# Moving a diagonal sum and a turned gradient off TensorE, into the last phase of a fused layer's kernel

## The chip, the cores and the metric

The kernel runs on one core of one Trainium2 chip. The core has a matrix engine (TensorE, PE in the profile), a vector engine (VectorE, DVE), a scalar engine (ScalarE, ACT), GpSimd (POOL), and a sequencer (SyncE, SP) that here only issues DMA transfers. Weight loads of TensorE have a row of their own (PEld). Matrix products land in PSUM; everything else works on SBUF, a memory of 128 partitions. The metric is the device time of one execution in microseconds (us), and lower is better. The kernel before takes 1876.19 us, the median of three runs between 1875.66 and 1876.70.

## The reference

The function computes a layer and all of its gradients. The input is normalised, and the normalised rows `xn` go into two branches whose results are added to the input: a long convolution over time (branch A) and a gated MLP (branch B). The part that the change touches belongs to the gradients of branch A:

```python
# S = 2048 time steps, D = 1024 channels, ks = 4 taps
k_pad = jnp.pad(k, ((0, 0), (ks - 1, 0), (0, 0)))
for t in range(ks):
    k_shift = k_shift + k_pad[:, t:t + S, :] * shift_k[:, ks - 1 - t][None, None, :]
kv = k_shift * v
# y = causal convolution of kv with ssm_k (a filter of S steps for each channel), by FFT
y = y + kv * ssm_D[None, None, :]
return q * y
# [cut: layer norm, the MLP; jax.vjp gives the gradients of q, k, v, shift_k, ssm_k, ssm_D and the weights]
```

Two of these gradients matter here. Call `gks` the gradient that reaches `k_shift`, with S rows and D columns.

- **The gradient of `shift_k`** (D x 4): for each channel and each tap i it is the sum over time of `gks[t] * k[t - i]`. These are the tap sums.
- **The gradient of `ssm_k`** (D x S): a filter gradient, one row of 2048 time steps for each channel. Branch A works with time on the partitions and channels along the free axis, so this output has to be turned. Its element at time 0 is also the gradient of `ssm_D`.

## The kernel before

The kernel has four stretches. In the first three (`hidden`, `grad_down`, `grad_in`) TensorE does the MLP's products, and branch A is woven into them: a generator of slots puts a few of branch A's TensorE instructions between the MLP's at set distances, one group of 128 channels after another, eight groups in all. Then `out_phase` computes the output, and `grad_x` the gradient of the input, in 16 row tiles of 128 time steps each.

The tap sums before were matrix products. For each of 16 sub-rows and each block of 32 channels, TensorE multiplies a 128 x 32 piece of `gks` by four shifted pieces of `k`. Only the diagonals of the 32 x 32 results are wanted; VectorE masks them with an identity and sums them.

```python
def tap_sums(self, st):
    gks, kp = st["gks"], st["kp"]
    pd = self.banks("h x")[1](0)[:, 0:P].rearrange("p (i c) -> p i c", i=4)
    for r in range(16):
        for b in range(0, P, 32):
            self.mm(pd[b:b + 32], gks[:, r, b:b + 32], kp[:, r:r + 4, b:b + 32], start=(r == 0), stop=(r == 15))
    st["pd"] = pd

def tap_diagonals(self, st):
    dg = self.tmp.tile([P, 4, 32], F32, name="dg", tag="tmp")
    self.tt(dg[:], st["pd"], self.ident32[:].to_broadcast([P, 4, 32]), ALU.mult)
    self.pri.late()
    self.pri.pin(self.nc.vector.tensor_reduce(out=self.gs_all[:, st["gi"], :], in_=dg[:], axis=AX.X, op=ALU.add))
```

The last step of an inverse transform exists in two forms. `inv_b` leaves time on the partitions: its stationary operand is the small table `RB`. `inv_b_chan` leaves channels on the partitions, so that the filter gradient can be stored as the output wants it: its stationary operand is the data, 32 pieces of 128 x 128.

```python
def inv_b(self, st, key, half):
    dst, Cf = self.ttile(key), self.flp[:, half]
    for j in range(2):
        ps, at = self.banks("h r c", r=8)
        for q in range(4):
            for e in range(2):
                rows, n0 = slice(64 * e, 64 * e + 64), 16 * (q // 2) + 8 * j
                self.mm(at(e)[32 * q:32 * q + 32], self.RB[rows, e, :],
                        Cf[rows, n0:n0 + 8, 64 * (q % 2):64 * (q % 2) + 64])
        self.evict(...)                       # [cut: view]

def inv_b_chan(self, st, half):
    dst, Cf = self.ttile("ghn"), self.flp[:, half]
    for n0 in range(0, NB1, 16):
        ps, at = self.banks("h n c", n=8)
        for n in range(16):
            self.mm(at(n // 8)[:, n % 8, :], Cf[:, n0 + n, :], self.RB[:].rearrange("p h n -> p (h n)"))
        self.evict(...)                       # [cut: view]

def store_gh(self, st):                       # [cut: views]
    self.vcopy(self.gD_all[:, :, st["gi"]:st["gi"] + 1], ghv[0:64, :, 0:1])
    for b in range(2):
        self.store(self.out_gh[...], ghv[64 * b:64 * b + 64])
```

After the last group, `small_outputs` turns the collected tap sums and `ssm_D` gradients with six TensorE transposes and stores them. The last phase looks like this:

```python
def grad_x(self, ...):
    p_ev = tc.alloc_tile_pool(name="x_ev", bufs=2, side="right")
    for st in range(self.ST):                           # 16 row tiles
        ggT = self.tall(ug_d[:, 1, :], st, "ggT")       # DMA transposes; these two share a pool of three buffers
        guT = self.tall(ug_d[:, 0, :], st, "guT")
        # [cut: loads of gt, gy, xn on SP]
        V.tensor_tensor(out=gy[:], in0=gy[:], in1=gt[:], op=ALU.mult)
        if st == 1:
            self.rest_load(x, xn_d, y_d, Wd)
        gx, pr, w = ...                                 # pr: 128 x 1024 bf16, two buffers
        for ob in range(2):
            ps = self.ps_tile("ps_x")                   # a pool of four PSUM banks
            for T, W in ((ggT, self.wgT), (guT, self.wuT)):
                for kt in range(self.FT):               # 28
                    nc.tensor.matmul(ps, lhsT=T[:, kt, :], rhs=W[:, kt, oc], start=..., stop=...)
            V.tensor_tensor_reduce(out=gx[:, oc], in0=ps, in1=gy[:, oc], ...)
            V.tensor_tensor_reduce(out=pr[:, oc], in0=gx[:, oc], in1=xn[:, oc], ...)
            # [cut: row statistics]
        # [cut: ScalarE scales xn, VectorE adds, SP stores the row tile]
    self.rest_out(h_d, out0)                            # a short rest of the output's products
```

Of the kernel before, what the change touches and what calls it, by code (L numbers as in the profile page):

```python
# [11 lines left out]
BF16 = mybir.dt.bfloat16  # L12
F32 = mybir.dt.float32
I32 = mybir.dt.int32
ALU = mybir.AluOpType
ACT = mybir.ActivationFunctionType
AX = mybir.AxisListType
P = 128
# [3 lines left out]
class Pri:  # L22
# [4 lines left out]
    def __init__(self, tc):  # L27
        self.tc = tc
        self.n = 0
        self.strict = False  # L30
# [15 lines left out]
NB1 = 32  # L46


class ABranch:
# [4 lines left out]

    def __init__(self, tc, pri, S, D, k, v, g, shift_k, ssm_k, ssm_D, xn_d, y_d, sk_d, out_gk, out_gv, out_gsk,
                 out_gh, out_gsD):
        assert S == 2048 and D % P == 0
        self.tc, self.nc, self.pri = tc, tc.nc, pri
        self.S, self.D, self.NG = S, D, D // P
        self.k, self.v, self.g, self.shift_k, self.ssm_k, self.ssm_D = k, v, g, shift_k, ssm_k, ssm_D  # L60
        self.xn_d, self.y_d, self.sk_d = xn_d, y_d, sk_d
        self.out_gk, self.out_gv, self.out_gsk, self.out_gh, self.out_gsD = out_gk, out_gv, out_gsk, out_gh, out_gsD
        self.pools, self.pin, self.dense, self.queue = [], False, False, []
        self.cap, self.turns = 2, 0
# [83 lines left out]
    def tables(self):  # L148
        nc, con, big, pri = self.nc, self.con, self.big, self.pri
        pri.late()  # L150
        V, hold = nc.vector, self.tc.keep_in_program_order
# [4 lines left out]
        self.RB = con.tile([P, 2, NB1], BF16, name="RB")  # L156
        self.gs_all = con.tile([P, self.NG, 4], F32, name="gs_all")
        self.gD_all = con.tile([64, 2, self.NG], BF16, name="gD_all")
        negpi = con.tile([P, 1], F32, name="negpi")
# [23 lines left out]
        for a in range(2):  # L183
            V.tensor_scalar(out=it[:, a, :], in0=it[:, a, :], scalar1=b5[:], scalar2=32.0 * (1 + a) + 64.0,
                            op0=ALU.mult, op1=ALU.add)
# [6 lines left out]
        for ri in range(2):  # L192
            off = lin(b32, -1024.0, 1024.0 * (1 + ri) + 2048.0, "offF%d" % ri)
            q = big.tile([P, NB1, NB1], I32, name="qF", tag="big")
# [40 lines left out]

        self.ident32 = con.tile([P, 1, 32], BF16, name="ident32")
        self.NX = con.tile([1, 3, P], BF16, name="NX")
        V.memset(self.NX[:], 0.0)
        for b in range(0, P, 32):
            V.tensor_copy(out=self.ident32[b:b + 32, 0, :], in_=self.identA[b:b + 32, b:b + 32])  # L240

# [80 lines left out]
    def load_taps(self, st):  # L322
        skb = st["skb"] = self.sm.tile([P, 4, 1, P], BF16, name="skb")
        self.load(skb[:].rearrange("p i o c -> p (i o c)"),
                  self.sk_d[4 * st["gi"]:4 * st["gi"] + 4, :].rearrange("i c -> (i c)").partition_broadcast(P))
# [173 lines left out]

    def inv_b_chan(self, st, half):  # L500
        dst, Cf = self.ttile("ghn"), self.flp[:, half]
        st["ghn"] = dst
        dv = dst[:, 0:16, :].rearrange("p r c -> p (r c)").rearrange("p (n1 n2) -> p n1 n2", n2=NB1)
        for n0 in range(0, NB1, 16):
            ps, at = self.banks("h n c", n=8)
            for n in range(16):
                self.mm(at(n // 8)[:, n % 8, :], Cf[:, n0 + n, :], self.RB[:].rearrange("p h n -> p (h n)"))
            self.evict(ps, "p h n c -> p c (h n)", lambda s: dv[:, :, n0 + 8 * s.start:n0 + 8 * s.stop])
        yield

    def store_gh(self, st):
        ghf = st["ghn"][:, 0:16, :].rearrange("p r c -> p (r c)")
        ghv = ghf.rearrange("p (h t) -> p h t", h=2)
        self.vcopy(self.gD_all[:, :, st["gi"]:st["gi"] + 1], ghv[0:64, :, 0:1])
        for b in range(2):
            self.store(self.out_gh[st["cg"], 1024 * b:1024 * b + 1024].rearrange("(h c) t -> c h t", h=2),
                       ghv[64 * b:64 * b + 64])

    def halo(self, st):
# [4 lines left out]
        self.load(gks[P - 1:P, 16:19, :], self.NX[0:1, 0:3, :])  # L524

    def tap_sums(self, st):

        gks, kp = st["gks"], st["kp"]
        pd = self.banks("h x")[1](0)[:, 0:P].rearrange("p (i c) -> p i c", i=4)
        for r in range(16):  # L530
            for b in range(0, P, 32):
                self.mm(pd[b:b + 32], gks[:, r, b:b + 32], kp[:, r:r + 4, b:b + 32], start=(r == 0), stop=(r == 15))
        st["pd"] = pd

    def tap_diagonals(self, st):
        dg = self.tmp.tile([P, 4, 32], F32, name="dg", tag="tmp")
        self.tt(dg[:], st["pd"], self.ident32[:].to_broadcast([P, 4, 32]), ALU.mult)
        self.pri.late()
        self.pri.pin(self.nc.vector.tensor_reduce(out=self.gs_all[:, st["gi"], :], in_=dg[:], axis=AX.X, op=ALU.add))

# [32 lines left out]
    def steps(self):  # L573
# [25 lines left out]
        for st in self.sts:  # L599
            for p, d in (self.wide_slots if self.dense else self.slots)(st, st["gi"]):  # L600
# [8 lines left out]
                yield self.DENSE[p is None] if self.dense else self.SLOT  # L609
        self.small_outputs()  # L610

# [60 lines left out]
    def slots(self, st, gi):  # L672
# [56 lines left out]
        yield None, lambda: self.tt(gv[:, 0:16, :], gkv[:, 0:16, :], st["ksh"][:], ALU.mult)  # L729
        self.store_time(self.out_gv, st["cg"], gv)  # L730
        yield None, q
        yield None, self.both(lambda: self.halo(st), q)
        yield lambda: self.tap_sums(st), None
        self.fetch(nx, self.load_k, self.load_taps)
        f1g = None
        if not last:
# [3 lines left out]
            f1g = self.fwd1(self.Bg, nx["gt"])  # L740
        yield None, lambda: self.tap_diagonals(st)
        ia = self.inv_a_pair()
# [40 lines left out]
        yield None, tk  # L783
        yield self.inv_b_chan(st, 1), tk
        yield None, tk
# [19 lines left out]
    def wide_slots(self, st, gi):  # L805
# [60 lines left out]
        yield None, lambda: self.tt(gv[:, 0:16, :], gkv[:, 0:16, :], st["ksh"][:], ALU.mult)  # L866
        self.store_time(self.out_gv, st["cg"], gv)
        yield None, q
        yield None, self.both(lambda: self.halo(st), q)
        yield lambda: self.tap_sums(st), None  # L870
        self.fetch(nx, self.load_k, self.load_taps)
        f1g = None
        if not last:
# [3 lines left out]
            f1g = self.fwd1(self.Bg, nx["gt"])  # L877
        yield None, lambda: self.tap_diagonals(st)
        ia = self.inv_a_pair()
# [41 lines left out]
        yield None, tk  # L921
        yield self.inv_b_chan(st, 1), tk
        yield None, tk
# [18 lines left out]

    def small_outputs(self):
        nc, NG = self.nc, self.NG
        tp = nc.tensor.transpose
        sk = self.sm.tile([P, NG, 4], BF16, name="sk_o", bufs=1)
        self.vcopy(sk[:], self.gs_all[:])
        ps = self.ps.tile([P, 1024], BF16, name="ps8", tag="aps")
        for i in range(4):
            self.pri.now()  # L950
            self.pri.pin(tp(ps[0:NG, i * P:(i + 1) * P], sk[:, :, 3 - i], self.identA[:]))
        for h in range(2):
            self.pri.now()
            self.pri.pin(tp(ps[0:NG, 4 * P + 64 * h:4 * P + 64 * h + 64], self.gD_all[:, h, :], self.identA[0:64, 0:64]))
        so = self.tmp.tile([NG, 5, P], BF16, name="so", tag="tmp")
        self.vcopy(so[:, 0:4, :].rearrange("g i c -> g (i c)").rearrange("g (c i) -> g i c", i=4),
                   ps[0:NG, 0:4 * P].rearrange("g (i c) -> g i c", i=4))
        self.vcopy(so[:, 4, :], ps[0:NG, 4 * P:5 * P])
        self.store(self.out_gsk.rearrange("(g c) i -> g (c i)", c=P), so[:, 0:4, :].rearrange("g i c -> g (i c)"))
        self.store(self.out_gsD.rearrange("(g c) -> g c", c=P), so[:, 4, :])  # L960
A_START = 60_000


class LnMlp:
# [741 lines left out]

    def grad_x(self, x, g, xn_d, y_d, h_d, ug_d, Wd, out0, out1):
        nc, tc, D, V = self.nc, self.tc, self.D, self.nc.vector
        p_ev = tc.alloc_tile_pool(name="x_ev", bufs=2, side="right")
        p_sm = tc.alloc_tile_pool(name="x_sm", bufs=2, side="right")  # L1710
        for st in range(self.ST):
            for _ in range(6):
# [11 lines left out]
            if st == 1:  # L1724
                self.rest_load(x, xn_d, y_d, Wd)
            gx = p_ev.tile([P, D], F32, name="gx")
            pr = p_ev.tile([P, D], BF16, name="pr")
# [32 lines left out]
        self.rest_out(h_d, out0)  # L1760
        self.p_rest.release()
        p_sm.release()
        p_ev.release()
# [7 lines left out]
def kernel(  # L1771
# [32 lines left out]
    ug_d = dram.tile([S, 2, F], BF16, name="ug_d")  # L1804

    sk_d = dram.tile([D // P * 4, P], BF16, name="sk_d")

    pri = Pri(tc)
    b = LnMlp(tc, pri, S, D, F)
    a = ABranch(tc, pri, S, D, A_k[0], A_v[0], g, A_shift_k, A_ssm_k, A_ssm_D, xn_d, y_d, sk_d[:], out_2[0], out_3[0],  # L1810
                out_4, out_5, out_6)
    b.open_left()
# [36 lines left out]
    b.out_phase(x, xn_d, y_d, h_d, B_W_gate, B_W_up, out_0[0])  # L1849
    b.grad_x(x, g, xn_d, y_d, h_d, ug_d, B_W_down, out_0[0], out_1[0])  # L1850

# [29 lines left out]
```

## Time and profile before

| | value |
|---|---|
| time, median of three | 1876.19 us |
| span of the profiled execution | 1874.5 us |
| granted TensorE clock | 1.0 |
| branch A woven into the MLP's products | to about 1244 us |
| `out_phase` | 1290 to 1478 us |
| `grad_x` | 1478 us to the end |
| tap sums, TensorE instructions | 512 products of 128 x 32 by 128 x 128 |
| turned filter gradient, TensorE instructions | 256 products of 128 x 128 by 128 x 64 |
| `inv_b`, for two other results | 256 products of 64 x 32 by 64 x 512 |

The page of a profile gives the busy time of each engine first, then the span in forty slices, the DMA queues, the chain of work that ended last, and the costliest groups of instructions. A group's mean is the duration of one instruction as the profiler saw it. Matrix products are pipelined, so the durations of neighbours overlap, and the distance between the starts of two is what one of them costs. The timeline lists instructions in order of time with the start and the length of each run of like ones. The table by stretches gives, for each stretch, the busy time of each engine with the number of its instructions, the granted clock, the mean busy share of the sixteen DMA engines (it can exceed 1, since packets overlap) and the GB/s that they moved.

### The profile page before, as it was taken

Reading aid. Unit: us, or ns where it says so; the run is one execution under the profiler, and the core shown is the slowest. Engines: PE = TensorE matmul, PEld = TensorE weight load, DVE = VectorE, ACT = ScalarE, POOL = GpSimd, SP = SyncE. Lnnn points to the kernel's source line nnn. Section 1 sums busy time; section 2 is a strip of 40 time slices with the busy share of each in tenths; the row PEclk is TensorE's granted clock in tenths of the full one; section 3 lists DMA queues with packets and bytes.
Section 4 is the critical chain, followed back from the end, with each engine's and each line's share of the span. In section 5 each row is a group of like instructions: output and inputs, shape, how many; then the busy total and the mean of one; then the engine's idle time right before and its main releaser. Section 6 shows DMA issues by size and latency. Waiting matters only on the chain.

```text
span 1874.5 us, 32572 instructions
## 1 busy us (share of the span) xinstructions
PE 1852.7 (99%) x13478; PEld 852.5 (45%) x13707; DVE 1050.2 (56%) x1537; ACT 613.1 (33%) x904; POOL 14.8 (1%) x37
## 2 busy tenths in 40 slices
PE   9999999999999999999999999999999999999999
PEld 4444444444444444444444444444444544444444
DVE  6656888699698677685585876710222222222222
ACT  5745444534445445444535454320000000000000
POOL 1000000000000000000000000000000000000000
PEclk9999999999999999999999999999999999999999
DMA  9897499868568747377465353479999945555553
GB/s 254 257 246 169 134 204 222 193 166 200 150 163 209 246 100 192 104 185 216 136 148 153 97 165 98 136 172 278 259 226 249 249 115 123 124 123 124 124 124 73
DMA packets 695509, 323.72 MB, mean 173 GB/s; under 512 B 524864, under 2 KB 664896, under 8 KB 695360
## 3 DMA queue, kind: packets, MB, share of 16 engines
q1 hardware_dynamic: 684864, 300.78, 65.1%
q10 hardware_dynamic: 9216, 16.65, 2.9%
q0 software_dynamic: 1280, 4.20, 0.6%
q8 instruction: 107, 1.75, 0.4%
q14 instruction: 42, 0.34, 0.1%
HBM read 143.79 MB, written 95.44 MB: 128 GB/s over the span
## 4 chain that ended last, share of the span: by engine, by line
PE 97%; issue 1%; DMA 1%; DVE 0%; SPq 0%; ACT 0%; POOL 0%; ACTq 0%; POOLq 0%
PE ps_x L1739 21%; PE ps_w L1503 20%; PE ps_u L1171 10%; PE ps_h L1171 10%; PE ps_o L1670 10%; PE ps_g L1171 10%; PE ps_d L1503 9%; PE ps L89 4%; PE ps_d L1518 1%; PE ps_c L89 1%; PE ps_w L1518 1%; PE ps_r L1700 0%; PE ps_warm L1226 0%; DMA wu<-in_B_W_up_dram 0%; SPq L1189 0%
## 5 line engine op out<-in xcount | busy, mean ns | idle before, releaser
L1503 PE MATMUL ps_w<-ugs,xn_nat 128*128 128x512 bf16 x1672 | 377.1, 380 | 4.5 <-issue 2.4
L1171 PEld LDWEIGHTS <-xnT 128*128 128x128 bf16 x1792 | 170.8, 98 | 208.9 <-issue 8.2
L93 ACT CAST arena<-ps 128x1024 bf16<-128x1024 f32 x240 | 234.3, 1021 | 72.2 <-PE ps L89 62.9
L1503 PEld LDWEIGHTS <-xn_nat 128*128 128x128 bf16 x1728 | 164.4, 98 | 201.3 <-issue 9.8
L344 DVE STREAM_TRANSPOSE arena<-arena 128x1024 f32<-128x1024 f32 x96 | 180.4, 1933 | 129.1 <-ACT arena L93 115.6
L1171 PE MATMUL ps_u<-wu,xnT 128*128 128x512 bf16 x875 | 205.3, 380 | 1.4 <-issue 0.3
L1171 PE MATMUL ps_g<-wg,xnT 128*128 128x512 bf16 x867 | 203.1, 380 | 2.4 <-issue 0.6
L1171 PE MATMUL ps_h<-wdT,goT 128*128 128x512 bf16 x862 | 202.8, 380 | 2.6 <-issue 0.8
L1757 ACT ACTIVATE w<-xn,m 128x512 f32<-128x512 bf16 x32 | 24.3, 806 | 553.0 <-issue 317.2
L1739 PE MATMUL ps_x<-wgT,ggT 128*128 128x512 bf16 x879 | 197.6, 379 | 0.9
L1739 PE MATMUL ps_x<-wuT,guT 128*128 128x512 bf16 x877 | 197.5, 379 | 1.0
L1670 PE MATMUL ps_o<-wd,hT 128*128 128x512 bf16 (+1 forms) x878 | 186.6, 373 | 0.9
L1503 PE MATMUL ps_d<-g_nat,hs 128*128 128x512 bf16 x740 | 168.8, 380 | 2.1 <-issue 0.8
L1739 PEld LDWEIGHTS <-guT 128*128 128x128 bf16 x896 | 87.7, 98 | 105.7
L1739 PEld LDWEIGHTS <-ggT 128*128 128x128 bf16 x896 | 87.7, 98 | 105.5
L1171 PEld LDWEIGHTS <-goT 128*128 128x128 bf16 x896 | 85.5, 98 | 105.4 <-issue 5.5
L1670 PEld LDWEIGHTS <-hT 128*128 128x128 bf16 x896 | 87.7, 98 | 100.0
L1506 ACT CAST wi<-ps_w 128x512 bf16<-128x512 f32 x108 | 63.8, 591 | 200.5 <-PE ps_w L1503 180.2
L1741 DVE CUSTOM_DVE_ANT_0 gx<-ps_x,gy 128x512 f32<-128x512 f32 x32 | 22.1, 692 | 185.3 <-PE ps_x L1739 175.4
L1413 ACT CAST gh<-ps_h 128x512 bf16<-128x512 f32 x112 | 65.5, 585 | 184.1 <-PE ps_h L1171 173.2
L1286 DVE SCALAR_TENSOR_TENSOR ru<-ru,ps_u 128x512 bf16<-128x512 bf16 x112 | 76.5, 684 | 81.9 <-PE ps_u L1171 44.4
L97 DVE TENSOR_TENSOR t<-arena 128x2048 bf16<-128x2048 bf16 x96 | 114.1, 1219 | 0.4
(165 smaller groups left out, 1341.6 us busy)
## 6 DMA issues: line engine op xcount, KB each, us to landing
ug_d<-ru SPq DMA_DIRECT2D x112, 256.0 KB
ugs<-ug_d SPq DMA_DIRECT2D x112, 256.0 KB
wg<-in_B_W_gate_dram SPq DMA_DIRECT2D x56, 256.0 KB
wu<-in_B_W_up_dram SPq DMA_DIRECT2D x56, 256.0 KB
h_d<-ht SPq DMA_DIRECT2D x112, 128.0 KB
hs<-h_d SPq DMA_DIRECT2D x56, 256.0 KB
out_dram<-wi SPq DMA_DIRECT2D x56, 256.0 KB
gt<-in_grad_out_dram SPq DMA_DIRECT2D x32, 256.0 KB
```

What stands on the lines that cost most here:

```text
L89: self.pri.pin(self.nc.tensor.matmul(out, lhsT=lhsT, rhs=rhs, start=start, stop=stop))
L93: self.pri.pin(self.nc.scalar.copy(out=out, in_=in_))
L97: self.pri.pin(self.nc.vector.tensor_tensor(out=out, in0=in0, in1=in1, op=op))
L344: self.pri.pin(self.nc.vector.transpose(out=df[:, c0:c0 + 32, :], in_=sf[:, c0:c0 + 32, :]))
L1171: self.pri.pin(self.nc.tensor.matmul(ps[:], lhsT=xT[:, kt * P:(kt + 1) * P], rhs=w(kt), start=(kt == 0), stop=(kt == self.DT - 1)), always ...
L1286: return self.pri.pin(nc.vector.scalar_tensor_tensor(out=ru[s][:, 1, :], in0=ru[s][:, 0, :], scalar=0.0, in1=ps[:], op0=ALU.is_gt, op1=ALU ...
L1413: self.pri.pin(nc.scalar.copy(out=gh[:], in_=ps[:]))
L1503: self.pri.pin(self.nc.tensor.matmul(ps[:], lhsT=lhsT(st), rhs=rhs(st), start=(st == 0), stop=(st == self.ST - 1)))
L1506: self.pri.pin(self.nc.scalar.copy(out=out, in_=ps[:]))
L1518: self.pri.pin(self.nc.tensor.matmul(ps[i][:], lhsT=lhsT(i, st), rhs=rhs(i, st), start=(st == 0), stop=(st == self.ST - 1)))
L1670: nc.tensor.matmul(ps, lhsT=hT[:, kt, :], rhs=self.wd[:, kt, oc], start=(kt == 0), stop=(kt == self.FT - 1))
L1739: nc.tensor.matmul(ps, lhsT=T[:, kt, :], rhs=W[:, kt, oc], start=(i == 0), stop=(i == n - 1))
```

## The change

The change takes the tap sums and the turning of the filter gradient off TensorE.

- In branch A, the tile `gks` is stored to a buffer in HBM, `gks_d`, as it lies: 128 partitions with 4 KB each. The filter gradient is computed by `inv_b` with time on the partitions and stored in the same way to `gh_d`. The gradient of `ssm_D` is then one row of that tile and is stored directly. The slots in which the tap sums stood stay in the generator, empty, so that the order of all else is kept.
- In `grad_x`, from the seventh row tile on, each of eight row tiles takes care of one group of channels. In the row tile before, three DMA transposes of 2048 x 128 elements bring `gks`, `k` and the filter gradient into SBUF with channels on the partitions. Then ScalarE puts the time steps of the filter gradient into order (four copies of 128 x 512), two transfers store it, and VectorE forms the four tap sums with eight multiply-and-sum instructions of 128 x 1024.
- `small_outputs`, the identity mask and the buffers for the diagonals go.

It is meant to leave TensorE only the work that needs it, and to use engines and DMA capacity that the last phase leaves idle.

```diff
+    def store_gh(self, st):
+        self.store(self.out_gsD[st["cg"]].rearrange("(o c) -> o c", o=1), st["gh"][0:1, 0, :])
+        self.store(self.gh_d[st["gi"]], st["gh"][:, 0:16, :].rearrange("p r c -> p (r c)"))
...                                     (both slots and wide_slots)
         self.store_time(self.out_gv, st["cg"], gv)
+        self.store(self.gks_d[gi], gks[:, 0:16, :].rearrange("p r c -> p (r c)"))
         yield None, q
         yield None, self.both(lambda: self.halo(st), q)
-        yield lambda: self.tap_sums(st), None
+        yield [], None
...
-        yield None, lambda: self.tap_diagonals(st)
+        yield None, None
...
-        yield self.inv_b_chan(st, 1), tk
+        yield self.inv_b(st, "gh", 1), tk
...
-        self.small_outputs()
...
+    TAPS_AT = 6
+
+    def open_taps(self):
+        self.p_tap = self.tc.alloc_tile_pool(name="x_tap", bufs=2, side="right")
+        self.p_gs = self.tc.alloc_tile_pool(name="x_gs", bufs=1, side="right")
+        self.gs = self.p_gs.tile([P, 2, self.DT, 4], F32, name="gs")
+
+    def load_taps(self, g, gks_d, gh_d, k):
+        flat = lambda d: d[g].rearrange("p (r c) -> (p r) c", c=P)
+        gksT = self.p_tap.tile([P, S], BF16, name="gksT")
+        nc.sync.dma_start_transpose(out=gksT[:], in_=flat(gks_d))
+        kT = self.p_tap.tile([P, 16 + S], BF16, name="kT")
+        nc.gpsimd.memset(kT[:, 0:16], 0.0)
+        nc.sync.dma_start_transpose(out=kT[:, 16:], in_=k[:, g * P:(g + 1) * P])
+        ghT = self.p_gs.tile([P, S], BF16, name="ghT")
+        nc.sync.dma_start_transpose(out=ghT[:], in_=flat(gh_d))
+
+    def taps(self, g, out_gh, pool):
+        for b in range(2):
+            gn = pool.tile([P, self.D], BF16, name="pr")
+            for u in range(2):
+                lo = u * h + b * (h // 2)
+                nc.scalar.copy(out=gn[:].rearrange("p (q u r) -> p q u r", u=2, r=16)[:, :, u],
+                               in_=ghT[:, lo:lo + h // 2].rearrange("p (q r) -> p q r", r=16))
+            nc.sync.dma_start(out=out_gh[g * P:(g + 1) * P, b * h:b * h + h], in_=gn[:])
+        for i in range(4):
+            ks = kT[:, 16 - i:16 - i + self.S].rearrange("p (q u r) -> p q u r", u=2, r=16)
+            for u in range(2):
+                junk = pool.tile([P, self.D], BF16, name="pr")
+                nc.vector.tensor_tensor_reduce(
+                    out=rows(junk), in0=rows(gksT[:, u * h:u * h + h]), in1=ks[:, :, u], scale=1.0, scalar=0.0,
+                    op0=ALU.mult, op1=ALU.add, accum_out=self.gs[:, u, g, i:i + 1])
...                                     (grad_x, after gy has been formed)
+            group = st - self.TAPS_AT
+            if 0 <= group < self.DT:
+                self.taps(group, out_gh, p_ev)
+            if group == self.DT:
+                self.store_taps(out_gsk)
+            if 0 <= group + 1 < self.DT:
+                self.load_taps(group + 1, gks_d, gh_d, k)
```

The new tiles `gn` and `junk` take turns in the same two buffers as `pr`.

## The prediction, as it was put on record before the changed kernel was seen

> **What bounds the kernel now.** I read the page's list of engines first, then the table by stretches, then timelines of the places that the change touches. The page and the table:
>
> ```profile
> PE 1852.7 (99%) x13478; PEld 852.5 (45%) x13707; DVE 1050.2 (56%) x1537; ACT 613.1 (33%) x904; POOL 14.8 (1%) x37
> ...
> PE 97%; issue 1%; DMA 1%; DVE 0%; SPq 0%; ACT 0%; POOL 0%; ACTq 0%; POOLq 0%
> ```
>
> ```profile
> 0.00:660.00 660.00, 651.52 (x5101) 296.88 (x5195) 504.96 (x790) 314.78 (x463) 13.15 (x33) 1.00 0.79 200
> 864.00:1290.00 426.00, 421.26 (x3712) 194.33 (x3769) 247.75 (x266) 177.62 (x269) 0.81 (x2) 1.00 0.55 155
> 1290.00:1478.00 188.00, 187.05 (x882) 87.87 (x899) 41.49 (x62) 0.58 (x1) 0.00 (x0) 1.00 1.12 241
> 1478.00:1865.00 387.00, 385.11 (x1761) 175.51 (x1795) 107.43 (x251) 22.78 (x30) 0.00 (x0) 1.00 0.53 125
> ```
>
> After the times and the length, the columns are PE, PEld, DVE, ACT and POOL busy, the clock, the DMA share and GB/s. TensorE sets the time in every stretch: it is busy in 651.5 of 660 us, in 385.1 of the last phase's 387, and 97% of the chain is its products. The other engines have room, most of all in the last phase: VectorE 107 of 387 us (28%), ScalarE 23 us (6%), DMA share 0.53. So the change can gain only by what it takes off TensorE's queue, and lose only by making TensorE wait.
>
> A busy sum does not say what an instruction costs on TensorE, since overlapping products are counted where they stand. I use distances of starts. In `grad_x` the same transfer recurs every 24.17 us (guT at 1568.93 and 1593.10, shown below), and a row tile has 112 products of 128x512, so one costs 24.17 / 112 = 0.2158 us.
>
> [...] a product is listed with 380 ns and costs 216. That is why I measure slots. [...] 16 products of 64x32 by 512 columns fill a slot of 0.65 us, where 16 full ones would take 3.45. [...] Here the transposes of the last phase run at 290 GB/s in windows of 1 us that hold nothing else. [...] The trace has 692 ns for 1024 bf16 elements and for 512 fp32 ones[...].
>
> **What leaves TensorE.** Three runs of the timeline of TensorE, with the MLP's products on both sides: tap sums, turned filter gradient, and the form that replaces it.
>
> ```profile
> 240.66 3.62 PE L1171 MATMUL ps_g<-wg,xnT 128*128 128x512 bf16 x15
> 244.21 1.08 PE L89 MATMUL ps<-kp,gks 128*32 128x128 bf16 x64
> 245.22 3.63 PE L1171 MATMUL ps_u<-wu,xnT 128*128 128x512 bf16 x15
> ```
>
> ```profile
> 299.97 3.62 PE L1171 MATMUL ps_g<-wg,xnT 128*128 128x512 bf16 x16
> 303.43 1.10 PE L89 MATMUL ps<-RB,arena 128*128 128x64 bf16 x32
> 304.36 1.89 PE L1171 MATMUL ps_u<-wu,xnT 128*128 128x512 bf16 x7
> ```
>
> ```profile
> 228.78 1.03 PE L1171 MATMUL ps_h<-wdT,goT 128*128 128x512 bf16 x4
> 229.74 0.62 PE L89 MATMUL ps<-arena,RB 64*32 64x512 bf16 x16
> 230.29 1.90 PE L1171 MATMUL ps_g<-wg,xnT 128*128 128x512 bf16 x8
> ```
>
> Each slot is the start of the block behind, minus the start of the block ahead, minus the products of that block at 0.2158.
> - Tap sums: 245.22 - 240.66 - 16 x 0.2158 (one record of 16 is missing) = 1.11 us. The other groups have the same 1.10, and the last one 1.32. Eight groups: 7 x 1.10 + 1.32 = 9.0 us, **gone**.
> - Turned filter gradient: 304.36 - 299.97 - 16 x 0.2158 = 0.94. Six groups have 0.93, two have 1.15: 7.9 us in all. `inv_b` in its place: 230.29 - 228.78 - 4 x 0.2158 = 0.65, eight times 5.2. **Saved: 2.7 us.**
> - The six transposes of `small_outputs`: the MLP's block at 1238.30 has 24 products, which end at 1243.48, and the next block starts at 1244.04. **Saved: 0.6 us.**
>
> The sum is 9.0 + 2.7 + 0.6 = 12.3 us. It comes off the time in full, because TensorE's queue is the chain there and the empty slots keep the spacing of the rest. VectorE loses some 0.75 us a group (mask 0.29, sum 0.29, copy 0.16); that lies beside TensorE and is worth nothing. The evictions by ScalarE stay: two of 128x1024, 1.03 us each.
>
> **What phase A gets.** Per group, one more store of 512 KB, and the filter gradient's store with 4 KB runs instead of two stores with 2 KB runs. Eight times 0.52 MB is 4.2 MB more; at the stretch's 200 GB/s some 21 us of DMA work spread over 1000 us whose share is 0.55 to 0.79. The waits for DMA there are small. I allow 0.3 us.
>
> **What the last phase gets.** SyncE's issues in one row tile, by the timeline of its queue:
>
> ```profile
> 1568.93 3.50 SPq L1636 DMA_TRANSPOSE guT<-ug_d  x1
> 1574.97 3.71 SPq L1636 DMA_TRANSPOSE ggT<-ug_d  x1
> 1578.78 0.52 SPq L1718 DMA_DIRECT2D gt<-in_grad_out_dram  x1
> 1579.75 0.82 SPq L1759 DMA_DIRECT2D out_dram<-o  x2
> 1580.62 0.46 SPq L1720 DMA_DIRECT2D gy<-y_d  x1
> 1581.17 0.38 SPq L1722 DMA_DIRECT2D xn<-xn_d  x1
> 1593.10 3.52 SPq L1636 DMA_TRANSPOSE guT<-ug_d  x1
> ```
>
> The reader is to see the hole: SyncE is done at 1581.55 and then stands until 1593.10 at the next guT, which waits for a buffer that TensorE frees three quarters into its row tile. That is 11.5 us of queue and, by the table in finer stretches, 9 us (1584 to 1593) with a DMA share of 0.01.
> - Queue: 8 blocks of 128x128 take 1.29 us to issue (xnT), 28 take 3.58 (guT), so 16 take 1.29 + 8 x 0.1145 = 2.21. Three new transposes 6.6, two stores 0.8: 7.4 us, into a hole of 11.5.
> - Data: 3 x 0.524 MB at 290 GB/s = 5.4 us, and 0.52 MB of stores at 240 GB/s 2.2 us: 7.6 us, into a hole of 9. `k` is read in pieces of 256 B at a pitch of 2 KB; wdT is read in much the same way (512 B pieces, same pitch) and issues as fast as the others.
> - Slack behind it: guT(st+1), issued at 1593.10, is first used at a quarter of the next row tile, 1574.7 + 24.2 + 6.0 = 1604.9. Its issue takes 3.5 us and its data lands about 5 us after the start, so it may come 6 to 7 us late before TensorE waits.
> - VectorE: a multiply-and-sum of 512 elements at 1x takes 692 ns; the fixed part is 158 (425 ns at 512 and 692 at 1024 bf16 elements). So 1024 elements take 158 + 2 x 534 = 1.23 us, with the 0.08 of the accumulator read 1.31, eight of them 10.5 us. With the 6.8 that a row tile has now, 17.3 of 24.2. The sums stand ahead of the eviction of `ps_x` in VectorE's queue and may hold it up by some 8 us; four PSUM banks are two row tiles, so TensorE does not see it.
> - ScalarE: four copies of some 0.6 to 0.8 us. Hidden.
>
> I expect a wait here of 0, at most some tenths of a us per row tile.
>
> **Rivals.** (A) *SyncE's queue blocks.* The stores of `gn` wait for ScalarE, which waits for `ghT`; `gn` also takes turns with `pr` in two buffers, so it waits for the epilogue of the row tile before. If the scheduler puts a store or a transpose so that it holds guT(st+1) until the end of the row tile, TensorE loses 2 to 4 us in each of 8 row tiles, 16 to 32 us: 1880 to 1896. For it: the queue is in order, and one buffer of `ghT` ties the next load to the copies. Against it: all these conditions are met before half of the row tile, and the hole is 11.5 us. (B) *The transposes are slow in DMA.* At half the rate they take 11 us instead of 5.4; total DMA 24 of 24 us, guT lands late, a few us per row tile: 1870 to 1890. For it: pieces of 256 B, and ggT's issue stretched to 5.24 us where transfers crowd. Against it: the transposes here run at 290 GB/s in the same pieces. (C) *Phase A's time is not TensorE's alone*, and a slot taken out turns into a wait for an eviction or VectorE. VectorE is busy 505 of 660 us. Then perhaps half of 12.3 arrives: 1870. Against it: TensorE stands still for only 8.5 of those 660 us.
>
> **Range and chances.** 1876.2 - 12.3 + 0.3 = 1864.2; for the last phase I add nothing. Some more saving is possible, where a change between kinds of product costs more than the slots show: low end 1860.5. Half of rival C or a small dose of A or B gives 1870 at the high end. Faster by 2% would need 1838.7, three times what leaves TensorE: 1%. Slower by 2% would need 1913.7, rival A at its worst: 3%.
>
> **What would show it right or wrong.** The profile after should have no products of `kp` with `gks`, eight more runs of sixteen 64x32 products, for `gh`, and the start of `grad_x` some 12 us earlier, at about 1466. The last phase should keep a row tile of 24.17 us, with guT's issue still at three quarters of it. If a row tile with taps is longer, A or B holds, and the idle time ahead of `ps_x` names the transfer. If `grad_x` starts later than 1468, C holds. VectorE's new instructions should last 1.2 us; at twice that I would be wrong by 10 us of VectorE time per row tile, its total 27.8 of 24.2 us, and the banks would fill after a few row tiles. The prediction is wrong most easily by an order of SyncE's queue that I could not see.

## The result, and the profile after

The changed kernel takes **1867.43 us**, the median of four runs between 1866.25 and 1868.93; beside it the kernel before took 1876.39. The ratio is 0.9953, with a 95% interval of 0.9936 to 0.9970. That is 9.0 us less; 12.0 had been predicted, and 1867.43 lies in the predicted range. The two profiled executions differ by as much: spans of 1874.5 and 1864.9 us, 9.6 less.

The page of the changed kernel, its list of engines, and the chain that ended last:

```profile
PE 1841.5 (99%) x12836; PEld 838.2 (45%) x13061; DVE 1115.7 (60%) x1635; ACT 630.3 (34%) x935; POOL 15.6 (1%) x45
...
PE 95%; SPq 2%; DMA 1%; issue 1%; DVE 0%; ACT 0%; ACTq 0%
```

TensorE lost 11.2 us of busy time and some 640 records, and is still 99% of the span. VectorE gained 65 us, which by themselves cost nothing that the last experiment below could measure. New is the 2% of SyncE's queue (SPq) in the chain: somewhere TensorE's work now hangs on the order in which transfers are issued.

The table by stretches for the last phase, some 10 us earlier than before and as long:

```profile
1466.00:1855.00 389.00, 386.11 (x1771) 176.45 (x1805) 180.71 (x381) 40.09 (x62) 0.83 (x8) 1.00 0.74 169
```

VectorE has 181 us here instead of 107, ScalarE 40 instead of 23, the DMA share is 0.74 instead of 0.53. TensorE is busy in all but 3 us.

The list of one tile's instructions, for the products into `ps_x` (durations, then the first and the last start), gives the start of `grad_x`:

```profile
L1741 PE MATMUL ps_x<-wgT,ggT x878: 378/379/380, 1467.7 to 1849.4; 128*128 128x512 bf16 x176
```

Before, it started at 1478.1. So **10.4 us were gained ahead of `grad_x`**, and `grad_x` itself became 0.8 us longer: 396.4 us before (1874.5 - 1478.1), 397.2 now (1864.9 - 1467.7). What TensorE waited for, by the view of waits (us in total, times, longest), is new above all in two lines:

```profile
PE ps_x L1741 <- DMA guT<-ug_d: 1.0, 1, 1.0
...
PE ps_u L1119 <- DMA wu<-in_B_W_up_dram: 0.4, 1, 0.4
```

**The gain.** The slot of the tap sums, in TensorE's timeline:

```profile
241.41 3.62 PE L1119 MATMUL ps_g<-wg,xnT 128*128 128x512 bf16 x15
244.87 3.62 PE L1119 MATMUL ps_u<-wu,xnT 128*128 128x512 bf16 x16
```

The two blocks of the MLP now stand 3.46 us apart, which is 16 products of 0.216 and nothing between. I matched the MLP's weight loads of the two traces one by one (they come in the same order) and read where their distance changes: by 1.11 us at each of the eight tap slots, 8.9 in all, and by 0.3 more once behind the first of them; by 0.258 at each turned gradient, 2.1 in all; by 0.57 at `small_outputs`. The sum is 11.8 us. Given back are 0.7 us in the first 60 us, where both kernels have the same instructions (the other runs lose between -0.5 and +3.1 us there), and 1.0 us at about 415 us, where TensorE stood for the weights `wu`: eight products take 2.80 us instead of 1.82, of which the view of waits counts 0.4 as one wait. That leaves 10.1 of the measured 10.4; I did not find the rest. SyncE's timeline shows why `wu` came late:

```profile
400.16 1.37 SPq L113 DMA_DIRECT2D gks_d<-gks  x1
401.58 1.39 SPq L1244 DMA_DIRECT2D h_d<-ht  x1
...
405.88 2.06 SPq L1112 DMA_DIRECT2D wg<-in_B_W_gate_dram  x4
...
409.94 2.10 SPq L1112 DMA_DIRECT2D wu<-in_B_W_up_dram  x3
```

The added store of `gks` occupies the queue for 1.37 us ahead of both weight loads. That it is its place in the queue and not its bytes that costs the time is what `own_late_gks` below tests.

**The wait for guT.** In the second row tile of `grad_x`, well before the first of the eight row tiles with new work (the tap tiles), SyncE issues guT:

```profile
1496.41 3.58 SPq L1636 DMA_TRANSPOSE guT<-ug_d  x1
```

That is the kernel before; the changed one:

```profile
1482.81 0.47 SPq L1634 DMA_DIRECT2D rest<-in_A_q_dram  x1
1483.32 4.75 SPq L1667 DMA_TRANSPOSE gksT<-gks_d  x1
1488.12 1.92 SPq L1670 DMA_TRANSPOSE kT<-in_A_k_dram  x1
1490.08 2.09 SPq L1672 DMA_TRANSPOSE ghT<-gh_d  x1
1492.27 4.56 SPq L1584 DMA_TRANSPOSE guT<-ug_d  x1
```

The program asks for group 0's transposes in the sixth row tile. Nothing they need ties them to it: their tiles are free and their data written long before. The scheduler put them here, in front of guT, behind the loads of `rest_load`. Before the change this guT was issued at 1496.4; moved by the 10.4 us gained it would come at 1486.0, and it comes at 1492.27, 6.3 us later. That used up the slack of 6 to 7 us which I had worked out, and, as the issue is slower too (4.56 us), one us more.

**The tap tiles.** One of them on SyncE's queue:

```profile
1618.09 0.53 SPq L1715 DMA_DIRECT2D gy<-y_d  x1
1620.24 1.90 SPq L1667 DMA_TRANSPOSE gksT<-gks_d  x1
...
1624.31 2.89 SPq L1670 DMA_TRANSPOSE kT<-in_A_k_dram  x1
1627.28 4.15 SPq L1685 DMA_DIRECT2D out_dram<-pr  x2
1632.30 3.85 SPq L1584 DMA_TRANSPOSE guT<-ug_d  x1
1636.19 2.02 SPq L1672 DMA_TRANSPOSE ghT<-gh_d  x1
```

Of the hole of 11.5 us ahead of guT about 1 us is left (1631.43 to 1632.30). The two stores of the ordered filter gradient (`out_dram<-pr`; `gn` in the code) hold the queue for 4.15 us where I had put 0.8, since the second waits for the copies of ScalarE, which wait for a buffer. In the first tap tiles guT still keeps its 24.17 us. From 1680.64 on it comes at 1705.81, 1731.24 and 1755.97, that is 25.2, 25.4 and 24.7 us apart: the queue has become slower than TensorE, and eats slack until the tap tiles end.

### The profile page after: what moved, and what is told of

Same layout as the page of the kernel before. It is cut to its first block, busy times and chain, and to the rows that moved or that the text cites. A ratio compares the mean times of both kernels' runs of the same rounds, so it can differ in the third digit from the quotient of the medians.

```text
span 1864.9 us, 31560 instructions
## 1 busy us (share of the span) xinstructions
PE 1841.5 (99%) x12836; PEld 838.2 (45%) x13061; DVE 1115.7 (60%) x1635; ACT 630.3 (34%) x935; POOL 15.6 (1%) x45
## 4 chain that ended last, share of the span: by engine, by line
PE 95%; SPq 2%; DMA 1%; issue 1%; DVE 0%; ACT 0%; ACTq 0%
PE ps_w L1451 20%; PE ps_x L1741 19%; PE ps_h L1119 10%; PE ps_u L1119 10%; PE ps_o L1618 10%; PE ps_g L1119 10%; PE ps_d L1451 9%; PE ps L89 4%; PE ps_d L1466 1%; PE ps_w L1466 1%; PE ps_c L89 1%; DMA wu<-in_B_W_up_dram 1%; DMA guT<-ug_d 0%; PE ps_r L1648 0%; SPq L1584 0%
## 5 line engine op out<-in xcount | busy, mean ns | idle before, releaser
L93 ACT CAST arena<-ps 128x1024 bf16<-128x1024 f32 x245 | 240.0, 1021 | 77.0 <-PE ps L89 70.2
L1451 PEld LDWEIGHTS <-xn_nat 128*128 128x128 bf16 x1728 | 164.6, 98 | 203.6 <-issue 11.5
L1610 DVE TENSOR_TENSOR ya<-ya,xe 128x1024 bf16<-128x1024 bf16 x16 | 11.1, 692 | 190.9 <-DMA xe<-xn_d 190.9
```

Source lines behind the costliest of these rows:

```text
L93: self.pri.pin(self.nc.scalar.copy(out=out, in_=in_))
L1451: self.pri.pin(self.nc.tensor.matmul(ps[:], lhsT=lhsT(st), rhs=rhs(st), start=(st == 0), stop=(st == self.ST - 1)))
```

## The experiments

Two theories of the missing 3 us and of the last phase were to be told apart. Mine: the gain is TensorE's slots alone, and what is missing comes from the order of SyncE's queue, at the three places above. The rivals: the new work of the last phase costs time by itself (DMA traffic, VectorE, PSUM banks), or the slots are worth less than their length.

### One half at a time, and the last phase left out

`taps_back` puts the tap sums back on TensorE, with the filter gradient turned by DMA as in the change:

```diff
-        self.store(self.gks_d[gi], gks[:, 0:16, :].rearrange("p r c -> p (r c)"))
-        yield [], None
+        yield lambda: self.tap_sums(st), None
-        gksT, kT, and the eight multiply-and-sums of a tap tile
+        tap_diagonals, small_outputs for the taps, as before
```

> The changed kernel with the tap sums back on TensorE in their old slots, and without the store of gks and without the sums and the two transposes for them in the last phase; the filter gradient is still turned by DMA. Theory (the gain is what leaves TensorE's queue, slot by slot): eight slots of 1.11 us return, 8.9 us, and four small transposes of about 0.4 us; two waits that the changed kernel shows (1.0 us for wu behind the store of gks, 1.2 us for guT behind three transposes) shrink or go. 1867.4 + 9.3 - 2 = about 1874.7 us. Rival (the transposes and sums of the last phase eat a good part of the gain): the time returns by less, 1868 to 1872 us.

Measured: 1874.14 us, median of 20 runs; ratio to the kernel before 0.9978 to 0.9992. `grad_x` starts at 1475.6, 7.9 us later than with the whole change. That is the eight tap slots (8.9), the 0.3 and 0.4 for four of the small transposes, less two losses of the changed kernel that this one does not have: the 1.0 us of waiting for `wu`, as it has no store of `gks`, and the 0.7 in the first 60 us, where it lost nothing.

`turn_back` puts back only the filter gradient:

```diff
-        yield self.inv_b(st, "gh", 1), tk
+        yield self.inv_b_chan(st, 1), tk
-        ghT, its transpose, the copies and the two stores of a tap tile
```

> The changed kernel with the filter gradient turned on TensorE as before and stored directly, and without its transposes, copies and stores in the last phase; the tap sums stay on VectorE in the last phase. Theory: eight slots are longer by 0.26 us, 2.1 us, and two small transposes return with some 0.4 us; the wait for guT loses one of three transposes ahead of it, up to 1.2 us less. About 1869 us. Rival (the stores of the turned gradient stand ahead of guT in SyncE's queue and cost TensorE time in every row tile): 1864 to 1866 us in spite of the longer slots.

Measured: 1869.14 us, four runs; 0.9944 to 0.9973. `grad_x` starts at 1469.0 instead of 1467.7. Without `gn` guT's issues stay 24.17 us apart through all tap tiles: it is the filter gradient's part (the transpose into ghT, the copies and the stores of `gn`) that stretches the queue, and not the tap sums alone. The wait for guT in the second row tile remained, 1.2 us.

`no_last_work` has branch A as changed and leaves out everything new in `grad_x`; the gradients of `shift_k` and `ssm_k` are not computed.

```diff
-            group = st - self.TAPS_AT
-            if 0 <= group < self.DT: self.taps(group, out_gh, p_ev)
-            ...                                          (store_taps, load_taps, open_taps)
```

> Branch A as in the changed kernel, but the last phase without the new transposes, copies, sums and stores: the gradients of shift_k and ssm_k are left out. Theory (the last phase hides all but one wait): only the wait of 1.2 us for guT in the second row tile goes; 1866.2 us, and the last phase takes 396.5 us as in the kernel before. Rival (the last phase pays in every row tile with taps, by SyncE's queue or DMA): 4 us or more come off, 1863 us or less.

Measured: 1865.82 us, four runs; 0.9923 to 0.9953. `grad_x` takes 396.0 us, 1.2 less than with its new work. So the new work of the last phase costs the changed kernel about 1 us in all, and the rest of the missing 3 lies ahead of `grad_x`, as my theory has it.

### The order of the transposes

`late_loads` ties the transposes to the load of `xn` in their row tile, so that they can't move to the front:

```diff
-            nc.sync.dma_start(out=xn[:], in_=xn_d[rows, :])
+            xl = nc.sync.dma_start(out=xn[:], in_=xn_d[rows, :])
-                self.load_taps(group + 1, gks_d, gh_d, k)
+                with tc.issue_after(xl.ins):
+                    self.load_taps(group + 1, gks_d, gh_d, k)
```

> The changed kernel, with the three transposes for a group held behind the load of xn of the row tile in which they stand, so that those of the first group no longer run in the second row tile, ahead of guT. Theory: the wait of 1.2 us for guT goes and nothing takes its place; 1866.2 us. Rival (the transposes of later groups, now tied to their places, crowd SyncE's queue ahead of guT in every row tile): 1868 us or more.

Measured: 1876.01 us, median of 12 runs; 0.9984 to 1.0001. **My expectation failed by 10 us**, and the rival's number, 1868 us or more, held. In the profiled execution 2.4 us of it lie in the first 60 us, where no instruction was changed; the rest is in `grad_x`. The wait in the second row tile was gone, but three others came in the tap tiles. The view of waits:

```profile
PE ps_x L1742 <- DMA guT<-ug_d: 6.1, 3, 3.2
```

SyncE's timeline of one turn:

```profile
1661.86 4.16 SPq L1584 DMA_TRANSPOSE guT<-ug_d  x1
...
1676.07 0.34 SPq L1713 DMA_DIRECT2D gt<-in_grad_out_dram  x1
1676.99 0.34 SPq L1762 DMA_DIRECT2D out_dram<-o  x1
...
1678.35 2.80 SPq L1667 DMA_TRANSPOSE gksT<-gks_d  x1
1681.24 2.35 SPq L1670 DMA_TRANSPOSE kT<-in_A_k_dram  x1
1683.68 4.26 SPq L1685 DMA_DIRECT2D out_dram<-pr  x2
1688.04 4.79 SPq L1584 DMA_TRANSPOSE guT<-ug_d  x1
```

guT now comes every 26.2 to 27.1 us, and VectorE and ScalarE show what holds it (in brackets the idle time ahead and what ended it):

```profile
1664.16 1.23 DVE L1691 CUSTOM_DVE_ANT_1 pr<-gksT,kT 128x1024 bf16<-128x1024 bf16 x1 [9.49 <-DMA out_dram<-pr]
```

```profile
1686.45 1.14 ACT L1683 COPY pr<-ghT 128x512 bf16<-128x512 bf16 x2 [8.48 <-DMA out_dram<-pr]
```

```profile
1690.70 1.23 DVE L1691 CUSTOM_DVE_ANT_1 pr<-gksT,kT 128x1024 bf16<-128x1024 bf16 x1 [9.07 <-DMA out_dram<-pr]
```

This is a **ring**. The sums can't start (9.49 us idle) until a store of `gn` has landed, since `junk`, `gn` and `pr` share two buffers. The row tile's epilogue stands behind the first sums in VectorE's queue, and `o` and `gt` behind the epilogue. The transposes, now tied to a place behind `gt`, are issued after these; the stores of `gn` come after the transposes, and the second of them again waits for a buffer that its own first store must free (8.48 us). When it has landed, the next sums start. The steps of the turn shown add up: sums and epilogue until `gt` 11.91 us, the loads and stores until gksT 2.28, two transposes 5.33, two stores 4.26, the landing 2.76, together 26.54 us from one first sum (1664.16) to the next (1690.70), where TensorE needs 24.17. In the changed kernel gksT is issued ahead of `o` and `gt`, and guT comes every 24.2 to 25.4 us; that the place of gksT is what makes its turn shorter is not shown by a run.

### Cutting the ring

`own_buffers` gives the sums' unused output the two buffers of `w`, and leaves the transposes where the change has them:

```diff
-                junk = pool.tile([P, self.D], BF16, name="pr")
+                junk = pool.tile([P, self.D], F32, name="w")[:].bitcast(BF16)
```

> The changed kernel, with the throw-away products of the tap sums written to the buffers of w instead of those of pr, so that only gn and pr still take turns. New theory (a ring: sums wait for the landing of the second gn store, the epilogue's loads wait for the sums, the two gn stores wait for the loads and for one another; about 24 to 27 us a turn, as long as a row tile): the ring is cut, guT is issued every 24.17 us at three quarters of the row tile through all the row tiles with taps, and VectorE no longer waits for the store. The wait for guT in the second row tile stays, so the time is that of the changed kernel, 1867.4 us within 1.5. Rival (SyncE's queue is simply full): the issues of guT still slip from 24.17 to 25.4 us.

Measured: 1869.64 us, four runs; 0.9948 to 0.9977. guT keeps its 24.17 us in all but one tap tile, where it comes 0.3 us late and makes it up in the next, and VectorE no longer waits for the store (34.4 us in all in the changed kernel), so the ring is cut. The edit did more than that, though. The scheduler ordered SyncE's queue anew, and in six of the eight tap tiles guT now stands between the two stores of `gn` and not behind both:

```profile
1684.29 0.53 SPq L1685 DMA_DIRECT2D out_dram<-pr  x1
1685.16 4.75 SPq L1584 DMA_TRANSPOSE guT<-ug_d  x1
1690.00 0.53 SPq L1685 DMA_DIRECT2D out_dram<-pr  x1
```

In the other two the queue still waits for ScalarE's copies between the stores (10.2 us in all, at most 5.6), but both stores are out 4 us or more before guT is issued. No run has the new buffers with the old order, so how much each of the two is worth stays open. The time missed my expectation, by the other defect: SyncE reached group 0's transposes 2 us later, and TensorE waited longer for guT in the second row tile:

```profile
PE ps_x L1741 <- DMA guT<-ug_d: 4.1, 1, 4.1
```

`own_late` has both edits.

> Both edits: transposes held behind xn, and the products of the sums in the buffers of w. Ring theory: with the ring cut, holding the transposes back no longer costs anything; the period of guT returns from 26.9 to 24.17 us, TensorE waits for it nowhere, and the time is 1866.2 us (1865 to 1867.5). Rival (the queue or DMA is too full when the transposes stand behind xn): 1870 us or more, with guT issues more than 24.17 us apart.

Measured: 1866.25 us, four runs; 0.9928 to 0.9962. No wait for guT is left, and guT stands between the two stores in six tap tiles here too. Each edit alone leaves TensorE waiting; the two together remove both waits.

`own_late_gks` also moves the added store of `gks` to a later place, behind the weight loads: five slots of the generator on, four in the last group (the expectation counts two).

```diff
-        self.store(self.gks_d[gi], gks[:, 0:16, :].rearrange("p r c -> p (r c)"))    (ahead of the empty tap slot)
         ...
         yield None, None
+        self.store(self.gks_d[gi], gks[:, 0:16, :].rearrange("p r c -> p (r c)"))
         ia = self.inv_a_pair()
```

> As the kernel with both edits, and the store of gks in branch A moved two slots on, behind the loads of wg and wu where they are near. Theory: the waits for wu at about 410 us, 1.0 us in all in the changed kernel, go as well: 1865.2 us. Rival (the waits come from the DMA load in that stretch as a whole and not from the place of the store): they move elsewhere, and the time is that of the kernel with both edits.

Measured: 1864.79 us, four runs; 0.9921 to 0.9950. The wait for `wu` is gone as well: all but 0.2 us of the 1.0, with the same bytes stored, which settles against the rival. This version beats both kernels.

### The two kernels side by side

`after_again` is the changed kernel without an edit, `best_again` is `own_late_gks`, on one chip.

> The changed kernel as it is, once more, for a comparison on one chip with the version that has the three edits. 1867.4 us within 1.5. If the early transposes are the hazard that they seem, TensorE waits again for guT in the second row tile, by 1 to 6 us from one execution to another, and for wu at about 410 us by some 1 us.

> The version with the three edits (transposes held behind xn, products of the sums in the buffers of w, store of gks two slots on), once more on the same chip. 1864.8 us within 1, that is 2 to 3 us below the changed kernel; no wait of TensorE for guT or wu, and a smaller spread of its times. If it was only the chip or chance: within 1 us of the changed kernel.

Measured: 1871.53 us (seven runs from 1868.51 to 1874.78; ratio 0.9957 to 0.9979) and 1865.47 (five runs from 1864.96 to 1866.31; 0.9922 to 0.9947). The better version is 6 us ahead, where I had expected 2 to 3: it came within 0.7 us of its expectation, and the changed kernel 4 us above its own. Beside the 1877.53 us of the kernel before on this chip, the change is worth 6.0 us and not the 9.0 of the first measurement, and 1871.53 lies above the range that I had predicted. The better version's `grad_x` starts at 1466.8 and takes 396.4 us, as long as that of the kernel before. The profile of `after_again` has waits of 3.0 us for guT in all, 1.5 in the second row tile and 0.8 and 0.7 in two late tap tiles:

```profile
PE ps_x L1741 <- DMA guT<-ug_d: 3.0, 3, 1.5
```

In the first execution shown above the tap tiles had no such wait; here guT comes 24.5 to 26.0 us apart in them. The profiled execution took 1868.96 us, so its waits do not account for the median; what the slower executions waited for is not shown. That the program stands at an edge where small differences of the transfers decide fits its wider spread; the version with the three edits has no wait and less spread.

### Twice the sums

`double_sums` is the changed kernel with each of the eight sums done twice, to see how far VectorE is from being a bound.

```diff
-                nc.vector.tensor_tensor_reduce(out=rows(junk), ...)
+                for _ in range(2):
+                    nc.vector.tensor_tensor_reduce(out=rows(junk), ...)
```

> The changed kernel with each of the eight sums of a row tile done twice, to the same place: 10.5 us more of VectorE's time in each of eight row tiles, 27.8 of 24.2 us. Ring theory: the ring becomes 34 to 37 us long and sets the pace; seven turns lose 10 to 12 us each, less some 7 us of slack ahead of guT: 1930 to 1945 us. The record's reading (VectorE's load against four PSUM banks): 8 x 3.6 us of overload less 24 us or more of slack in the banks, 1867 to 1880 us.

Measured: 1876.94 us, median of 18 runs; 0.9996 to 1.0010. The ring theory's number was far off. The scheduler ordered the queues anew (guT now stands ahead of gksT and of both stores), so this run does not test the ring that I had in mind. The number of the prediction's reading held, but not its reason; TensorE waited for transfers and not for PSUM banks:

```profile
PE ps_x L1742 <- DMA guT<-ug_d: 7.5, 4, 3.3
PE ps_x L1742 <- DMA ggT<-ug_d: 1.0, 1, 1.0
```

So the same doubling was put on the version without the ring, `double_sums_late`.

> The version with the three edits, with every sum done twice: VectorE's queue holds 27.8 us of work in each of eight row tiles of 24.17. If VectorE's lag reaches TensorE only by the four PSUM banks (the record's reading), 8 x 3.6 = 29 us of lag against 24 us or more in the banks: 1864 to 1872 us, and what TensorE waits for is VectorE. If the lag reaches TensorE by SyncE's queue, as in the first doubling (loads that wait for VectorE stand ahead of guT), TensorE waits for guT in the last of these row tiles: 1872 to 1880 us.

Measured: 1865.46 us, two runs; 0.9916 to 0.9952. TensorE has no listed wait for VectorE, DMA or banks in `grad_x`; guT stands ahead of gksT and both stores here as well. In a tap tile of VectorE's timeline:

```profile
1718.69 1.22 DVE L1692 CUSTOM_DVE_ANT_1 w<-gksT,kT 128x1024 bf16<-128x1024 bf16 x1
1719.84 0.08 DVE L1692 DVE_READ_ACCUMULATOR2_ANT gs<- 128x1 f32 x1
1719.84 1.22 DVE L1692 CUSTOM_DVE_ANT_1 w<-gksT,kT 128x1024 bf16<-128x1024 bf16 x1
```

Neighbouring sums start 1.15 us apart, since the read of the accumulator and the next sum overlap, so sixteen take 18.3 us, and VectorE's whole row tile about 24.7 us. It falls behind by half a us per row tile, and the banks hold that for eight. Eight more sums in each of eight row tiles, 74 us of VectorE's time, cost less than can be measured here. In this order the sums are free; what costs time is the queue and the buffers that they share.

## Why the prediction came out as it did

- **TensorE bounds every stretch, and only what leaves its queue counts: right.** `no_last_work` and `taps_back` came within 0.6 us of the expectations, which were worked out from slots and waits.
- **Tap slots 9.0 us: right** (8.9). **`small_outputs` 0.6: right** (0.57).
- **Turned gradient 2.7 us: mis-sized**, 2.1 by the traces. I counted two old slots at 1.15 us and took all of that down to 0.65; 0.258 is what a single slot gives, in those two as in the others. The extra 0.2 us there was a gap that stayed when the products changed.
- **0.3 us allowed for phase A's transfers: too little** by 0.7. I counted the bytes of the added store and the DMA share, which indeed did no harm. The term that failed is the issue time of the store (1.37 us) in a queue where weight loads stand behind it. Moving the store behind them, with the same bytes, ended the wait but for 0.2 us. Rival C is out: the slots arrived in full. My sign for it, a start of `grad_x` after 1468, was too fine: seven traces with the same branch A have starts from 1467.4 to 1470.0.
- **"I expect a wait here of 0": failed by 1 us** in the profiled execution, at two points. First, I took for granted that the transposes run in the row tile that asks for them. Group 0's, whose operands and buffers were free, were issued four row tiles early (gksT at 1483.32), ahead of guT (1492.27). My slack of 6 to 7 us was about right: 6 us of delay became 1 us of waiting. Second, I wrote against rival A that "all these conditions are met before half of the row tile". They were not: the stores of `gn` stand right ahead of guT, and their ring of shared buffers takes as long as a row tile. The term is "two stores 0.8": they hold the queue for 4.15 us, and with three transposes of 6.7 to 8.8 (estimate 6.6) the hole of 11.5 is full. In the profiled execution it only ate the slack; in `after_again` it cost two waits of 0.7 and 0.8 us, and in `late_loads` three of 1.3, 1.5 and 3.2. Rival A was therefore real in kind, and its 16 to 32 us too large for this order. I had named the shared buffers and not followed the ring once around.
- **The transposes' rate (rival B)** is not the bound. In the changed kernel the transposes into gksT and ghT mostly take 1.7 to 2.1 us to issue (estimate 2.21), those into kT 2.9 to 4.5 in the tap tiles, and the one in the crowd of the second row tile 4.75; the kernel with the same transposes in better places loses nothing. My 290 GB/s was the fastest of four windows of one transfer (118, 276, 290 and 234), so a whole transfer is slower than I had put it.
- **VectorE's sums 1.23 us each: right** (1.22), and the copies of ScalarE 0.61. The "1x" of the estimate is the rate of the 128x512 multiply-and-sum in the kernel before, 692 ns. The 1.31 us with the accumulator read was too long, as it overlaps: 1.15 apart when back to back. "TensorE does not see it" holds.

The terms' sum, for the profiled pair (9.6 us where 12.0 were predicted): the turned gradient 0.6, the first 60 us 0.7, `wu` 0.7 and `grad_x` 0.8 less than predicted make 2.8; the 0.3 behind the first tap slot and the 0.3 that I did not find go the other way. That leaves 2.2 of the 2.4 us. The 0.7 at the start is tied to no part of the change. That the first measurement fell inside the predicted range was in part luck: the second, 1871.53 us, fell outside it.

## What to carry to other kernels

When work moves to idle engines, its price is in the queues and buffers it joins: write down what stands behind each new transfer in its queue (here weight loads behind a store of 1.37 us, and guT behind three transposes of 8.8), and follow each shared buffer around once, adding up the times, to see whether that ring is shorter than the loop it lives in. A transfer without a dependence can land in another place of the queue, as group 0's did here, four row tiles early, so tie it to where it should stand, and give scratch outputs buffers that no store has to empty. And test the two repairs together: here each alone left TensorE a wait of 3 us or more, and only both removed the waits.

## What was not expected of the hardware

In three of these runs a wait of TensorE cost more than its length. In `late_loads` the table by stretches (PE busy, clock, DMA share, GB/s) around the wait of 3.2 us:

```profile
1746.00:1748.00 2.00, 0.00 (x0) 0.85 1.22 264
1748.00:1750.00 2.00, 1.48 (x4) 0.50 1.02 213
1750.00:1752.00 2.00, 2.00 (x6) 0.50 1.03 220
1752.00:1754.00 2.00, 2.00 (x6) 0.50 1.24 289
```

The clock fell to half at 1747.4, 2.1 us after the last product, and stayed there until 1754.2, 6.8 us in all; products ran from 1748.5 on: 5.7 us at half speed, 2.8 lost. With the 6.1 us of waits that makes 8.9, and `grad_x` there took 405.4 us (1875.4 - 1470.0), 9.0 more than the 396.4 of `best_again`. In `own_buffers`, after 4.1 us of waiting, the clock fell only 1.2 us after the products had resumed, and for 3.4 us. In `double_sums`, after a wait of 3.3 us, the products resumed at 1769.1, and the mean clock of 1770 to 1775 was 0.66, which is 3.4 us if it was at half. The shorter waits for transfers in `grad_x` did not bring the clock down: behind each of the nine of 0.7 to 1.8 us in `late_loads`, `double_sums` and `after_again` the 28 products into `ps_x` took 6.2 us, as without a wait, and behind those of 3.2 and 3.3 us they took 9.01 and 7.90. What sets the moment of the drop and its length, no run here tested.
